# A fused Mamba-2 scan and gated feed-forward: three of Strassen's seven products placed between the first products of the next step

## The chip, the cores and the metric

The kernel runs on one core of a Trainium2 chip. The metric is the device time of one execution in microseconds (us); the median of three runs is used. A profile of one further execution shows each instruction on each engine: PE is TensorE's matmul, PEld its weight load, DVE VectorE, ACT ScalarE, POOL GpSimd, SP the queue that issues most transfers.

## The reference

Two blocks follow one another. The first is a chunked state-space scan (batch 4, 8 heads, 768 positions, head size 32, state size 16). Its output is laid out as 3072 tokens of 256 features and goes into a feed-forward block with a cosine gate:

```python
x = np.ascontiguousarray(attn_out.transpose(0, 2, 1, 3)).reshape(B * S, H * D)
h = x @ w_in             # (3072, 256) @ (256, 2048)
g = h * np.cos(h)
return (g @ w_out).astype(np.float32)   # (3072, 2048) @ (2048, 256)
```

All of it is fp32. The feed-forward block is nearly all of the matmul work, and the change lies in its second product.

## The kernel before

**Tiling.** The sequence is cut into 6 chunks of 128 positions (NC), so a chunk holds 4 x 128 = 512 tokens. The 2048 inner features are 16 blocks of 128 (NF). The main loop (L739) counts steps n, 16 a chunk and 96 in all, and two more to drain (LAG is 2). From chunk 1 on, a step takes half of the chunk's tokens (u = 0 or 1: 256 of them) and two of the inner blocks (a pair j of 8). So eight consecutive steps share one u, and build up one set of outputs.

**A step.** `first(n)` (L502) makes h for step n in one PSUM bank, `hp`: four products (L512), e for the two inner blocks and k for the two halves of the contraction, each a 128x128 stationary matrix against 256 moving columns. ScalarE then makes the whole turns `k` (L516) and VectorE the remainder `w` (L518), both issued in `first`; `gate(n)` lets ScalarE take the sine (L523), and `gated(n)` lets VectorE multiply (L528) into `gT`, which also frees `hp`. There are two `hp` banks. For the Strassen product GpSimd then makes four differences of gT's blocks in `differ` (L549): d0 and d1 by L553, d2 by L555, d3 by L556.

**The second product.** `second(n - LAG)` (L560) runs two steps later. In chunk 0 it is a plain product (L571). From chunk 1 on it calls `seven` (L581): gT is a 2x2 arrangement of 128x128 blocks (two token halves, two inner blocks), w_out's rows of the pair another (two inner blocks, two output halves), and Strassen's scheme in Winograd's form needs seven 128x128x128 products (L609) in place of eight. Products 1, 2 and 4 take gT's own blocks; product 3 takes d3, 5 takes d0, 6 takes d2, 7 takes d1. They come in the order 1, 2, 6, 7, 5, 4, 3, and each adds over the eight steps into a place of its own in two PSUM banks: 1, 6 and 2 in `lo`, 7, 5, 4 and 3 in `hi`. `start` is set for the first product in each bank, since it begins the bank anew.

**The accumulators.** Both banks are made anew at j = 0 from the tag "o", of which there are two. So the next set takes the banks of the one just finished, and each may be written only when its copy to SBUF is done: at j = 7 ScalarE copies `lo` (L618) and VectorE copies `hi` (L619), and GpSimd combines them in four additions (L624). The very last set lies in three banks (`mid`, `lo`, `hi`), and `shared` and `last_step` (L632, L644) finish it.

**What sets the order.** The program is scheduled by hand: each engine runs its instructions in the order in which the code issues them. In one turn of the loop that is `first(n)`, in some steps the scan's transposes (`turn2`), `gate`, `gated`, then `second(n - LAG)` with, at j = 7, the copies, and then the scan's work for the chunk to come (`intra2`, `finish2` on TensorE; `masked`, `decays`, `reaches` on VectorE). So TensorE runs four first products, then seven Strassen products; ScalarE runs k(n), the sine of n, and then the copy L618 where there is one; VectorE runs w(n), gT(n), the copy L619, then the scan.

Of the kernel before, what the change touches and what calls it, by code (L numbers as in the profile page):

```python
# [25 lines left out]
def kernel(  # L26
# [35 lines left out]
    NC = S // P  # L62
    DM, DF = moe_w_in.shape
    KT = DM // P
    NF = DF // P
# [4 lines left out]
    LAG = 2  # L70
# [15 lines left out]
    def bank(shape, name, tag):  # L86
        return psum.tile(shape, FP32, tag=tag, bufs=2, name=name)

    def pair(name):

        return psum.tile([P, 2, 4 * P], FP32, tag="scan", bufs=2, name=name)
# [405 lines left out]
    def turn_of(n):  # L497

        c, f = divmod(n, NF)
        return (f % 2, f // 2) if c == 0 else divmod(f, NJ)  # L500

    def first(n):  # L502
        c, f = divmod(n, NF)
        hp[n] = bank([P, TB], "hp", "h")

        u, j = turn_of(n)
        to_ = hp[n].rearrange("p (e t s i) -> p e t s i", e=2, t=2, s=2)
        y = yT[c].rearrange("p k (u s t i) -> p k u t s i", u=2, s=2, t=2)
        for e in range(2):
            fs = slice((2 * j + e) * P, (2 * j + e + 1) * P)  # L510
            for k in range(KT):
                PE.matmul(to_[:, e], lhsT=w_in[:, k, fs], rhs=y[:, k, u],  # L512
                          start=(k == 0), stop=(k == KT - 1), skip_group_check=True)

        k = ffn.tile([P, TB], I32, tag="k", name="k")
        ACT.activation(k, hp[n], AF.Copy, bias=0.25, scale=INV_2PI)  # L516
        turns[n] = w = ffn.tile([P, TB], FP32, tag="w", name="w")
        V.scalar_tensor_tensor(out=w, in0=hp[n], scalar=INV_2PI, in1=k,  # L518
                               op0=ALU.mult, op1=ALU.subtract)

    def gate(n):
        cos = turns[n]
        ACT.activation(cos, cos, AF.Sin, bias=quarter, scale=TWO_PI)  # L523
# [35 lines left out]

    def second(n):  # L560
        c, f = divmod(n, NF)
        if c > 0:
            seven(n)
            return
        u, j = turn_of(n)
        if j == 0:
            o[c, u] = bank([P, 2, DM], "o", "o")
        g = gT.pop(n)
        for e in range(2):
            for t in range(2):  # L570
                PE.matmul(o[c, u][:, t], lhsT=g[:, 2 * e + t], rhs=w_out[:, 2 * j + e],  # L571
                          start=(j == e == t == 0), stop=(j == NJ - 1 and e == 1),
                          skip_group_check=True)
        if j < NJ - 1:
            return
        ob = conv.tile([P, 2, DM], FP32, tag="last", bufs=3, name="ob")
        (ACT.copy if u else V.tensor_copy)(out=ob, in_=o[c, u])
        for s in range(2):
            nc.sync.dma_start(out=to_rows[2 * u + s, c], in_=ob[s * W:(s + 1) * W])

    def seven(n):  # L581

        c = n // NF
        u, j = turn_of(n)
        final = n >= NC * NF - NJ
        if j == 0:


            if final:
                lo, hi = (pair("o")[:, 0].rearrange("p (q m) -> p q m", m=P) for _ in range(2))  # L590
                mid = bank([P, 4, P], "o", "o")
                o[c, u] = (mid, lo, hi, {1: mid[:, 0], 6: mid[:, 1], 7: mid[:, 2], 5: mid[:, 3],
                                         2: lo[:, 0], 3: lo[:, 1], 4: hi[:, 0]})
            else:
                lo, hi = (bank([P, 4, P], "o", "o") for _ in range(2))
                o[c, u] = (lo, hi, {1: lo[:, 0], 6: lo[:, 1], 2: lo[:, 2], 7: hi[:, 0],
                                    5: hi[:, 1], 4: hi[:, 2], 3: hi[:, 3]})
        at = o[c, u][-1]
        g = gT.pop(n)
        if n == NC * NF - 1:  # L600
            last_step(g, *o[c, u][1:3])
            return
        d = gd.pop(n)
        w = {1: w4[:, j, 0, 0], 2: w4[:, j, 1, 0], 3: w4[:, j, 1, 1], 4: wd[3][:, j],
             5: wd[0][:, j], 6: wd[2][:, j], 7: wd[1][:, j]}
        a_ = {1: g[:, 0], 2: g[:, 2], 3: d[:, 3], 4: g[:, 3], 5: d[:, 0], 6: d[:, 2], 7: d[:, 1]}
        starts = (1, 2, 4) if final else (1, 7)
        for q in (1, 2, 6, 7, 5, 4, 3):
            PE.matmul(at[q], lhsT=a_[q], rhs=w[q], start=(j == 0 and q in starts),  # L609
                      stop=(j == NJ - 1), skip_group_check=True)  # L610
        if final and j == NJ - 2:
            shared(o[c, u][0])
        if j < NJ - 1:
            return

        sum_ = two.tile([P, 7, P], FP32, tag="sum", bufs=1, name="sum")
        ps = two.tile([P, 7, P], FP32, tag="ps", bufs=1, name="ps")
        ACT.copy(out=ps[:, 0:3], in_=o[c, u][0][:, 0:3])  # L618
        V.tensor_copy(out=ps[:, 3:7], in_=o[c, u][1])  # L619
        for dst, a_, b_ in ((sum_[:, 0:2], ps[:, 1:3], ps[:, 0:1]),  # L620
                            (sum_[:, 5:7], ps[:, 3:5], sum_[:, 0:1]),
                            (sum_[:, 3:5], ps[:, 5:3:-1], sum_[:, 5:6]),
                            (sum_[:, 2:3], ps[:, 6:7], sum_[:, 6:7])):
            G.tensor_tensor(out=dst, in0=a_, in1=b_.to_broadcast([P, dst.shape[1], P]), op=ALU.add)  # L624
        for s in range(2):
            nc.sync.dma_start(out=to_rows[2 * u + s, c],
                              in_=sum_[s * W:(s + 1) * W, 1:5].rearrange(
                                  "p (t h) m -> p t (h m)", t=2))
# [15 lines left out]
    def last_step(g, lo, hi):  # L644

        for t, acc in enumerate((lo, hi)):
            for e in range(2):
                PE.matmul(acc[:, 0:2], lhsT=g[:, 2 * e + t], rhs=w_out[:, NF - 2 + e],
                          start=False, stop=(e == 1), skip_group_check=True)
            ob = conv.tile([P, 2, P], FP32, tag="last", bufs=3, name="ob")  # L650
            V.tensor_tensor(out=ob, in0=acc[:, 0:2], in1=shares_[t], op=ALU.add)
            for s, eng in enumerate((nc.sync, nc.scalar)):
                eng.dma_start(out=to_rows[NB - 2 + s, NC - 1, :, t],
                              in_=ob[s * W:(s + 1) * W].rearrange("p h m -> p (h m)"))
# [54 lines left out]
    def first_scan():  # L709

        finish(3, "o")
        for u in range(2):
            sums[u] = pair("s_ps")[:, :, 0:2 * D]
            for t in range(2):
                sum_up(0, 2 * u + t, sums[u][:, t])
# [12 lines left out]
    def pairs(n):  # L728

        at = [(1 + (n - t) // NF, u) for u, t in enumerate(TURN) if (n - t) % NF == 0]  # L730
        return [(c, u) for c, u in at if 0 < c < NC]
# [7 lines left out]
    for n in range(NC * NF + LAG):  # L739
        c, f = divmod(n, NF)  # L740
        early = n < EARLY
        if n < NC * NF:
            if f == 0 and c > 0:
                load(c + 2)
            first(n)
            if n == 0:
                first_scan()
            for at in pairs(n):
                turn2(*at)
            rests = [grade(*piece[m], later=True)  # L750
                     for m in ((n,) if early else ()) + ((n + 1,) if n >= EARLY - 1 else ())
                     if m in piece]
            gate(n)
            for rest in rests:
                if rest:
                    rest()
            if not early and n in piece:
                join(*piece[n])
            gated(n)
            if early and n in piece:  # L760
                join(*piece[n])
            if n in (1, 2):
                carry(0, n - 1, sums[n - 1])
        for i, js in differ_at.get(n, ()):
            differ_w(i, js)
        if n >= LAG:
            second(n - LAG)
        for c, u in pairs(n - 1):
            intra2(c, u)
            masked(c, 2 * u)  # L770
        for c, u in pairs(n - 2):
            masked(c, 2 * u + 1)
        for c, u in pairs(n - 3):
            finish2(c, u)
            if u == 1:
                raw.pop(c)
        for c, b, t in halves_at(n):
            decays(c, b, t)
            if t == 1:
                load_a(c + 1, (b,))  # L780
        for c, u in pairs(n + 1):
            for b in (2 * u, 2 * u + 1):
                reaches(c, b)
                load_along(c + 1, (b,))
# [30 lines left out]
```

## Time and profile before

| | value |
|---|---|
| time, median of 3 runs | 387.14 us (386.27 to 387.29) |
| span of the profiled execution | 384.9 us |
| PE busy | 378.3 us, 2982 instructions |
| PEld busy | 331.2 us |
| DVE / ACT / POOL busy | 265.9 / 172.9 / 245.4 us |
| L512, first products | 768 instructions, 383 ns each |
| L609, Strassen products | 1106 instructions, 274 to 277 ns each |
| L553, L555, L556 GpSimd differences | 79 each; 911, 546, 455 ns |
| L516 k, L518 w, L523 sine, L528 gT | 96 each; 595, 681, 722, 691 ns |

An fp32 product is two matmul instructions and two weight loads, so four first products are eight instructions and seven Strassen products fourteen. The duration of a matmul instruction is longer than the distance to the next, since they are pipelined; distances are read from starts in the timeline or from the chain of waits, which counts each instruction up to the start of the next. In the chain each entry is what the one after it waited for or followed on its engine, traced back from the end.

### The profile page before, as it was taken

How to read it: one execution, taken by the hardware profiler on the slowest of the kernel's cores; microseconds unless marked ns; L12 is line 12 of the kernel's file. 1: busy time of each engine (PE TensorE's matmuls, PEld its weight loads, DVE VectorE, ACT ScalarE, POOL GpSimd, SP SyncE). 2: the span in 40 equal slices, each digit the busy share in tenths (PEclk: the TensorE clock that was granted, in tenths of full speed). 3: DMA queues.
4: the chain of work that ended last, by engine and by line, in shares of the span. 5: the costliest groups of instructions: out<-in, count | busy, mean ns of one | idle time of the engine just before them, and what ended most of it. 6: DMA issues, size and time to landing. Idle time of an engine off the chain costs nothing.

```text
span 384.9 us, 7726 instructions
## 1 busy us (share of the span) xinstructions
PE 378.3 (98%) x2982; PEld 331.2 (86%) x2982; DVE 265.9 (69%) x395; ACT 172.9 (45%) x303; POOL 245.4 (64%) x366
## 2 busy tenths in 40 slices
PE   8999999999999999999999999999999999999996
PEld 3578887888899899899899899899899989989995
DVE  7879999678667658657657757756765865863443
ACT  3878566534334334335334434434433433433441
POOL 5757665458859549648648837855955855853751
PEclk9999999999999999999999999999999999999999
DMA  7989899975002951301791301201210000010001
GB/s 83 270 235 266 249 230 137 181 96 151 2 0 63 148 52 57 96 2 54 127 81 55 97 2 56 81 17 43 68 43 1 21 10 0 2 27 3 7 22 27
DMA packets 106371, 30.42 MB, mean 79 GB/s; under 512 B 75520, under 2 KB 102240, under 8 KB 106336
## 3 DMA queue, kind: packets, MB, share of 16 engines
q1 hardware_dynamic: 106176, 29.81, 38.9%
q8 instruction: 23, 0.38, 0.5%
q10 hardware_dynamic: 160, 0.13, 0.1%
q14 instruction: 12, 0.10, 0.1%
HBM read 26.59 MB, written 3.34 MB: 78 GB/s over the span
## 4 chain that ended last, share of the span: by engine, by line
PE 82%; DVE 7%; POOL 3%; ACT 2%; issue 2%; DMA 2%; SPq 1%; ACTq 0%
PE hp L512 37%; PE o L609 32%; PE g L422 3%; PE y L454 3%; DVE mag L209 2%; DVE w L518 2%; DMA xr<-in_x_dram 2%; PE y L447 2%; DVE lam L344 2%; PE o L571 1%; DVE gT L528 1%; PE warm L101 1%; ACT w L523 1%; PE a_ps L298 1%; PE tp L405 1%
## 5 line engine op out<-in xcount | busy, mean ns | idle before, releaser
L512 PE MATMUL hp<-yT,w_in 128*128 128x256 f32 x768 | 184.4, 383 | 0.6 <-POOL w_in L217 0.3
L512 PEld LDWEIGHTS hp<-yT,w_in 128*128 128x128 f32 x768 | 139.2, 190 | 22.7 <-issue 4.5
L553 POOL TENSOR_TENSOR gd<-gT 128x256 f32<-128x256 f32 x79 | 71.9, 911 | 89.5 <-DVE gT L528 86.2
L528 DVE TENSOR_TENSOR gT<-hp,w 128x512 f32<-128x512 f32 x96 | 66.3, 691 | 69.9 <-ACT w L523 60.1
L523 ACT ACTIVATE w<-w,quarter 128x512 f32<-128x512 f32 x96 | 69.3, 722 | 97.2 <-DVE w L518 97.2
L516 ACT ACTIVATE k<-hp 128x512 int32<-128x512 f32 x96 | 57.1, 595 | 90.8 <-PE hp L512 90.7
L518 DVE SCALAR_TENSOR_TENSOR w<-hp,k 128x512 f32<-128x512 f32 x96 | 65.4, 681 | 36.7 <-ACT k L516 36.4
L609 PE MATMUL o<-words,gd 128*128 128x128 f32 x474 | 67.0, 277 | 0.6 <-POOL gd L555 0.6
L609 PEld LDWEIGHTS o<-words,gd 128*128 128x128 f32 x474 | 59.3, 192 | 2.4 <-POOL gd L555 2.2
L344 DVE TENSOR_TENSOR_SCAN lam<-arow,unit 128x512 f32<-128x512 f32 x40 | 55.7, 1394 | 0.0
L609 PEld LDWEIGHTS o<-w_out,gT 128*128 128x128 f32 x316 | 46.9, 191 | 3.6
L609 PE MATMUL o<-w_out,gT 128*128 128x128 f32 x316 | 48.0, 274 | 0.0
L555 POOL TENSOR_TENSOR gd<-gT,gd 128x128 f32<-128x128 f32 x79 | 43.1, 546 | 6.2
L556 POOL TENSOR_TENSOR gd<-gT,gd 128x128 f32<-128x128 f32 x79 | 35.9, 455 | 6.2
L571 PE MATMUL o<-w_out,gT 128*128 128x256 f32 x128 | 30.3, 380 | 0.4 <-POOL w_out L217 0.4
L609 PE MATMUL o<-w_out,gd 128*128 128x128 f32 x158 | 30.6, 275 | 0.0
L609 PE MATMUL o<-words,gT 128*128 128x128 f32 x158 | 30.5, 275 | 0.0
L571 PEld LDWEIGHTS o<-w_out,gT 128*128 128x128 f32 x128 | 24.2, 190 | 4.0 <-POOL w_out L217 0.8
L435 DVE TENSOR_TENSOR m<-g,lam 128x512 f32<-128x512 f32 x40 | 25.6, 681 | 0.0
L624 POOL TENSOR_TENSOR sum<-ps,sum 128x256 f32<-128x256 f32 (+1 forms) x27 | 24.2, 909 | 1.4
L609 PEld LDWEIGHTS o<-w_out,gd 128*128 128x128 f32 x158 | 24.0, 192 | 0.0
L609 PEld LDWEIGHTS o<-words,gT 128*128 128x128 f32 x158 | 24.0, 192 | 0.0
(91 smaller groups left out, 293.9 us busy)
## 6 DMA issues: line engine op xcount, KB each, us to landing
arow<-a_cut SPq DMA_DIRECT2D x20, 512.0 KB
words<-in_moe_w_in_dram SPq DMA_DIRECT2D x8, 512.0 KB
words<-in_moe_w_out_dram SPq DMA_DIRECT2D x8, 512.0 KB
out_dram<-sum SPq DMA_DIRECT2D x18, 128.0 KB
xr<-in_x_dram SPq DMA_DIRECT2D x4, 512.0 KB
along<-a_all SPq DMA_DIRECT2D x20, 64.0 KB
xr<-in_x_dram SPq DMA_DIRECT2D x8, 128.0 KB
bc<-in_B_dram SPq DMA_DIRECT2D x4, 256.0 KB
```

The lines of the kernel that those rows point to most:

```text
L344: V.tensor_tensor_scan(out=lam[c, b][:, hs].rearrange("p h i -> p (h i)"), data0=rows_.rearrange("p h i -> p (h i)"), data1=unit.rearrange ...
L435: V.tensor_tensor(out=of[0], in0=g[q][:, :, s * 2 * P:(s + 1) * 2 * P], in1=of[1], op=ALU.mult)
L512: PE.matmul(to_[:, e], lhsT=w_in[:, k, fs], rhs=y[:, k, u], start=(k == 0), stop=(k == KT - 1), skip_group_check=True)
L516: ACT.activation(k, hp[n], AF.Copy, bias=0.25, scale=INV_2PI)
L518: V.scalar_tensor_tensor(out=w, in0=hp[n], scalar=INV_2PI, in1=k, op0=ALU.mult, op1=ALU.subtract)
L523: ACT.activation(cos, cos, AF.Sin, bias=quarter, scale=TWO_PI)
L528: V.tensor_tensor(out=gT[n], in0=hp.pop(n), in1=cos, op=ALU.mult)
L553: G.tensor_tensor(out=d[:, 0:2], in0=g[:, 1:2].to_broadcast([P, 2, P]), in1=g[:, 3::-3], op=ALU.subtract)
L555: G.tensor_tensor(out=d[:, 2], in0=g[:, 0], in1=d[:, 0], op=ALU.subtract)
L556: G.tensor_tensor(out=d[:, 3], in0=g[:, 2], in1=d[:, 2], op=ALU.subtract)
L571: PE.matmul(o[c, u][:, t], lhsT=g[:, 2 * e + t], rhs=w_out[:, 2 * j + e], start=(j == e == t == 0), stop=(j == NJ - 1 and e == 1), skip_gr ...
L609: PE.matmul(at[q], lhsT=a_[q], rhs=w[q], start=(j == 0 and q in starts), stop=(j == NJ - 1), skip_group_check=True)
```

## The change

`seven` becomes a generator. It gives way after each of products 1, 2 and 4, which now come first; `first(n)` takes it as `between` and runs a part of it after its second, third and fourth product. So TensorE's order is: first products (e, k) = (0, 0), (0, 1), then product 1 of step n - 2, first product (1, 0), product 2, first product (1, 1), product 4. The parts left over (products 7, 5, 6, 3, and at j = 7 the copies and sums) run where `second` stood. The three products need only gT and weights, not GpSimd's differences of gT, and the order of the others changes too. Since product 4 is now the first in `hi`, `start` goes from 7 to 4. Making the new banks at j = 0 is in the generator's first part, so it comes between the first products as well. Steps of chunk 0 and the last two of the loop are not woven. The change is meant to keep TensorE in work with products that are ready early, and to ask later for those that wait for GpSimd.

```diff
-    def first(n):
+    def first(n, between=()):
+
+        between = iter(between)
...
                 PE.matmul(to_[:, e], lhsT=w_in[:, k, fs], rhs=y[:, k, u],
                           start=(k == 0), stop=(k == KT - 1), skip_group_check=True)
+                if e or k:
+                    next(between, None)
...
     def second(n):
         c, f = divmod(n, NF)
-        if c > 0:
-            seven(n)
-            return
...
-        starts = (1, 2, 4) if final else (1, 7)
-        for q in (1, 2, 6, 7, 5, 4, 3):
+        starts = (1, 2, 4) if final else (1, 4)
+        for q in (1, 2, 4, 7, 5, 6, 3):
             PE.matmul(at[q], lhsT=a_[q], rhs=w[q], start=(j == 0 and q in starts),
                       stop=(j == NJ - 1), skip_group_check=True)
+            if q in (1, 2, 4):
+                yield
...
-            first(n)
+            weave = seven(n - LAG) if n - LAG >= NF else iter(())
+            first(n, weave)
...
-        if n >= LAG:
+        if LAG <= n < NF + LAG:
             second(n - LAG)
+        else:
+            for _ in weave if n < NC * NF else seven(n - LAG):
+                pass
```

## The prediction

> **What bounds the kernel now.** I read the page's shares first, then the chain of waits in the Strassen stretch, the list of waits, and the timeline of one place where the accumulators change hands. From the page:
>
> ```profile
> PE 378.3 (98%) x2982; PEld 331.2 (86%) x2982; DVE 265.9 (69%) x395; ACT 172.9 (45%) x303; POOL 245.4 (64%) x366
> ...
> PE 82%; DVE 7%; POOL 3%; ACT 2%; issue 2%; DMA 2%; SPq 1%; ACTq 0%
> ```
>
> TensorE is busy for 98% and is 82% of the chain. From the chain of waits between 200 and 260 us (start, us, what):
>
> ```profile
> 237.22 1.73 PE hp L512 x8
> 238.95 1.56 PE o L609 x14
> ...
> 244.24 1.73 PE hp L512 x8
> 245.97 1.81 PE o L609 x14
> ```
>
> One step is 8 first-product instructions in 1.73 us (216 ns each) and 14 Strassen instructions in 1.56 us (111 ns each; the fp32 product is two instructions), 3.29 us together with no hole. The second pair holds the only kind of hole: 1.81 for 14 instructions, 0.25 too many. The list of waits names it (us in total, times, longest):
>
> ```profile
> PEld o L609 <- POOL gd L555: 2.2, 9, 0.8
> PE o L609 <- POOL gd L555: 0.6, 1, 0.6
> ```
>
> These are waits of product 6, third of the seven, for GpSimd's second difference. Every wait also costs the pipelining of the next pair: six instructions of L609 take 0.94 us after one, 0.83 without, so 0.1 us is added. By the timeline the holes are 0.83 us at 94.5, 0.25 at seven later places (125, 155, 185, 246, 277, 307, 337), 0.28 at 209 (this one is for VectorE's copy L619) and 0.31 at 216: 0.83 + 1.75 + 0.59 = 3.17 us. That is all that there is to win.
>
> Now the place where one set of accumulators is emptied and the next is begun (timeline, start us, us, engine):
>
> ```profile
> 235.76 0.60 ACT L516 ACTIVATE k<-hp 128x512 int32<-128x512 f32 x1 [1.21 <-PE hp L512]
> ...
> 236.39 0.69 DVE L518 SCALAR_TENSOR_TENSOR w<-hp,k 128x512 f32<-128x512 f32 x1
> ...
> 237.06 1.89 PE L512 MATMUL hp<-yT,w_in 128*128 128x256 f32 x8
> ...
> 237.12 0.72 ACT L523 ACTIVATE w<-w,quarter 128x512 f32<-128x512 f32 x1 [0.76 <-DVE w L518]
> ...
> 237.74 0.46 ACT L618 COPY ps<-o 128x384 f32<-128x384 f32 x1
> ...
> 238.55 0.68 DVE L619 COPY ps<-o 128x512 f32<-128x512 f32 x1
> ...
> 238.79 0.61 PE L609 MATMUL o<-w_out,gT 128*128 128x128 f32 x4
> ```
>
> ScalarE's copy L618 empties the first bank at 238.20, and the next product 1 needs that bank at 238.79. So the wait is hidden today, with 0.59 us to spare, only because the whole of `first` stands ahead of product 1. The second bank is free at 239.23, after product 1 has begun: each bank is waited for by itself. There are nine such places:
>
> ```profile
> L618 ACT COPY ps<-o x9: 457/460/461, 116.2 to 358.5; 128x384 f32<-128x384 f32 x9
> ```
>
> **What the skill says.** "TensorE: Matmul & The Clock Gate", section "Step-by-step: what each phase is for": matmuls keep program order and only weight loads are pulled ahead; so first products behind a waiting product wait too. The trace agrees: behind the late product 6 everything slips. The same page, "LDWEIGHTS (loading the stationary operand)", gives columns/1.2 ns, an estimate of 107 ns for 128 columns; the trace has 111 ns per small instruction, so these are already at the pace of the loads. "Perfetto Trace Analysis", "Tensor Engine Instruction (MATMUL, LD_WEIGHTS)", calls ScalarE and VectorE strict FIFO: the copy L618 can't pass the sine L523 ahead of it, and the trace shows it 0.62 us after that sine's start at every place.
>
> **The change part by part.**
>
> *Weaving by itself.* The same 22 instructions per step, the same loads. A small one costs 111 ns beside small ones, a large one 216. In the timeline of single starts the first small one after a large one is 109 after it began, the first large one after small ones 218: two more changes of size a step are -3 + 2 ns each, under 0.2 us over 78 steps. I take zero.
>
> *Products 1 and 2 inside `first`.* They put 2 x 2 x 111 = 0.446 us ahead of the last first product, so hp ends 0.446 us later in its step, and so do k, w, sine, gT and GpSimd's differences of that step. These have slack in the steady state: gT frees hp at 237.94 + 0.69 = 238.63 by the same timeline, and the bank is written again two steps after 233.77, at 240.35: 1.7 us to spare.
>
> *The accumulators' handover.* Before, product 1 came after 8 large instructions; now after 4, at 237.06 + 0.86 = 237.92. The copy L618 comes 0.446 later, since k, w and the sine ahead of it in ScalarE's and VectorE's queues do: it ends at 238.20 + 0.45 = 238.65. A product starts some 0.05 us after its releaser ended (GpSimd 215.59 + 0.46 = 216.05, product at 216.10). So product 1 starts at 238.70: a hole of 0.78 us, and 0.1 for the lost pipelining, 0.88. Behind it in TensorE's queue stand the other half of `first` and all that follows, and nothing takes up the hole. Nine times: 7.9 us. Product 4, first into the second bank, comes some 1.4 us after product 1, at 240.1; copy L619 ends at 239.23 + 0.45 = 239.68, so no second hole. With no latency the hole is 0.73, with 0.2 us of latency and pipelining apart 1.03: 6.6 to 9.3 us.
>
> *The first woven step* has its first bank free, but product 4 needs the bank of L577 (ScalarE, 86.23 + 0.57 = 86.79) at 84.61 + 1.73 + 0.45 = 86.79: about 0.15 us lost.
>
> *The new order 1, 2, 4, 7, 5, 6, 3.* Product 6 moves from 1.73 + 0.45 = 2.17 us into the step to 2.17 + 3 x 0.22 = 2.84, 0.67 later, while the differences are 0.45 later: 0.22 us more slack, against waits of 0.15 to 0.21. Product 7 comes 0.22 later than product 6 did, and needs the difference of L553, which is ready 0.53 (0.45 of L555 and a gap) before that of L555: 0.3 more. At the wait of 94.5 GpSimd is held by L547, not by the shifted chain; there the move is worth 0.67 to product 6 and more to 7. So I take all 3.17 us as won.
>
> *The end.* `last_step` waits for gT(95), whose chain starts at the last first product's end: 0.446 later, and all behind it: 0.45 us lost. Product 6's later place delays the shared sums by 0.22 us, beside `last_step`'s 1.9 us of products: nothing.
>
> Sum: 7.9 + 0.15 + 0.45 - 3.17 = +5.3 us; 387.14 + 5.3 = 392.5 us.
>
> **The rivals.**
>
> 1. *No new hole* (the bank is free early enough after all, if ScalarE's copy moved ahead or the wait were taken elsewhere): only the gain, 387.14 - 3.17 + 0.6 = 384.6, or 384.0 if the end is hidden too. For it: 0.59 us of slack today. Against it: the product moves up by 0.86 us and the copy down by 0.45. Chance 0.14; this is the side of faster.
> 2. *A half hole*: the chain's shift is taken up somewhere (k, w and sine of that step not later). Hole 0.78 - 0.45 + 0.1 = 0.43, nine times 3.9: 387.14 + 3.9 + 0.6 - 3.17 = 388.5. Against it: k starts 0.1 us after the last first product, w and sine 0.03 us after their inputs, so there is no slack to take it up. Chance 0.08.
> 3. *The old waits stay* (VectorE and GpSimd slow each other: L553 is 0.72 to 1.58 us): the holes cost 8.5 and nothing is won, 395.7. Chance 0.08.
> 4. *Product 1 waits for both banks*: until L619 at 239.68 + 0.05, a hole of 1.8 + 0.1, nine times 17: about 401.8. Against it: product 1 at 238.79 did not wait for L619's end at 239.23. Chance 0.05.
>
> **How the numbers follow.** My forecast has 0.65, its bounds (6.6 to 9.3 us, gains half lost) 390.5 to 395.5. The range 388.3 to 396.0 takes in rivals 2 and 3 and leaves out 1 and 4. Faster 0.14, from rival 1; same 0.04, from between rivals 1 and 2; slower 0.82.
>
> **What would show it.** In the trace of after: the list of waits should name TensorE's L609 waiting for ACT ps L618 nine times, about 0.8 us each, and the chain should run through L523 and L618 there; the waits for L555 should be gone; a woven step without a handover should take 3.29 us as before; `last_step` should wait some 0.45 us. I am wrong if the handover shows no hole, or if steps between handovers are no longer 3.29 us, as they would be if alternating sizes changed the pace of the loads.

## The result, and the profile after

The changed kernel takes 391.68 us (median of 4 runs, 391.33 to 392.77) against 387.07 us for the kernel before on the same occasion: 1.0127 times as long, with a 95% interval of 1.0102 to 1.0153, which is 3.9 to 5.9 us. The forecast was 392.5.

From the page of the changed kernel, its shares of the span and the chain by engine:

```profile
PE 377.9 (97%) x2982; PEld 329.9 (85%) x2982; DVE 266.6 (68%) x395; ACT 174.9 (45%) x303; POOL 245.3 (63%) x366
...
PE 67%; DVE 14%; ACT 9%; issue 4%; DMA 3%; SPq 2%; POOL 0%; DVEq 0%; ACTq 0%
```

The instructions and TensorE's busy time are those of before, but TensorE is now 67% of the chain and not 82%; ScalarE has gone from 2% to 9% and VectorE from 7% to 14%. GpSimd, 3% before, is out of it. The list of waits of the changed kernel (total, times, longest) says which wait came in:

```profile
PEld o L611 <- ACT ps L622: 9.1, 9, 1.0
...
PE o L611 <- ACT ps L622: 5.5, 9, 0.6
```

L611 is what was L609, L622 what was L618. Nine waits, one for each set of accumulators that is emptied; the waits for GpSimd's L555 (now L559) are gone from the list; one of 0.2 us for L560, the difference of product 3, is new. One of the nine in the timeline of the changed kernel (start us, us, engine), at the same step as the place shown of before:

```profile
237.13 0.60 ACT L520 ACTIVATE k<-hp 128x512 int32<-128x512 f32 x1 [1.21 <-PE hp L514]
...
237.76 0.69 DVE L522 SCALAR_TENSOR_TENSOR w<-hp,k 128x512 f32<-128x512 f32 x1
...
237.99 1.03 PE L514 MATMUL hp<-yT,w_in 128*128 128x256 f32 x4
...
238.49 0.72 ACT L527 ACTIVATE w<-w,quarter 128x512 f32<-128x512 f32 x1 [0.76 <-DVE w L522]
...
239.11 0.46 ACT L622 COPY ps<-o 128x384 f32<-128x384 f32 x1
...
239.63 0.49 PE L611 MATMUL o<-w_out,gT 128*128 128x128 f32 x2 [0.61 <-ACT ps L622]
...
239.92 0.68 DVE L623 COPY ps<-o 128x512 f32<-128x512 f32 x1
...
240.38 0.38 PE L611 MATMUL o<-w_out,gT 128*128 128x128 f32 x2
```

Two first products (four instructions) end their turn at 237.99 + 4 x 0.216 = 238.86; product 1 starts at 239.63, since the copy ends at 239.57. VectorE's copy L623 ends only at 240.60, so it is not the one that product 1 waited for. The hole is 0.77 us, and the pair takes 0.49 and not 0.38: 0.88 in all.

Where the time went can be read from starts in the timeline, step by step (a step reaches from one first product's start to the next one's). I take it from step 18, the first that is woven, to TensorE's end:

| part | before to after, us |
|---|---|
| eight handovers, 3.29 to 4.17 each | +7.04 |
| the ninth (step 50), 3.57 to 4.24, of which 0.28 was there before | +0.67 |
| step 18 | +0.21 |
| from the start of step 95 to TensorE's end, 6.91 to 7.36 | +0.45 |
| step 20, 5.28 to 4.71 | -0.57 |
| eight steps two after a handover (28, 36, ... 84): seven of -0.24 to -0.26, one of -0.31 | -2.06 |
| sum; measured 296.58 to 302.27 | +5.74; +5.69 |

All other steps have their old length. The 5.7 us stand beside 4.6 in the medians and 4.7 in the two profiled spans, because step 18 began at 83.67 us in the profile of after and at 84.62 in that of before. The code up to there is the same, and in the profiles of all kernels below that start lies between 83.67 and 85.18. The scatter comes from the very beginning: from step 0 to step 18 each of these nine profiles takes 65.82 to 65.86 us, while step 0 begins between 17.85 and 19.32. The first matmuls of the program (L101, six that multiply ones) show it, before and then after:

```profile
1.06 4.63 PE L101 MATMUL warm<-ones 128*128 128x512 f32 x6 [1.06 <-DVE ones L96]
...
1.06 3.89 PE L101 MATMUL warm<-ones 128*128 128x512 f32 x6 [1.06 <-DVE ones L96]
```

In both, the second and third start 853 or 854 ns before the next; the fifth starts 426 ns before the sixth in the first profile and 217 in the second, so there TensorE had come to twice the pace sooner. I therefore compare the kernels from step 18 on where the difference is small.

### The profile page after: what moved, and what is told of

Same layout as the page of the kernel before. It is cut to its first block, busy times and chain, and to the rows that moved or that the text cites. A ratio compares the mean times of both kernels' runs of the same rounds, so it can differ in the third digit from the quotient of the medians.

```text
span 389.6 us, 7726 instructions
## 1 busy us (share of the span) xinstructions
PE 377.9 (97%) x2982; PEld 329.9 (85%) x2982; DVE 266.6 (68%) x395; ACT 174.9 (45%) x303; POOL 245.3 (63%) x366
## 4 chain that ended last, share of the span: by engine, by line
PE 67%; DVE 14%; ACT 9%; issue 4%; DMA 3%; SPq 2%; POOL 0%; DVEq 0%; ACTq 0%
PE hp L514 29%; PE o L611 23%; DVE lam L344 6%; DVE w L522 5%; ACT w L527 5%; PE g L422 3%; PE o L572 3%; PE y L454 3%; SPq L119 2%; ACT k L520 2%; PE y L447 2%; DMA words<-in_moe_w_out_dram 1%; DVE gT L532 1%; DMA arow<-a_cut 1%; PE tp L405 1%
## 5 line engine op out<-in xcount | busy, mean ns | idle before, releaser
L514 PE MATMUL hp<-yT,w_in 128*128 128x256 f32 x768 | 210.3, 383 | 0.6 <-POOL w_in L217 0.3
L514 PEld LDWEIGHTS hp<-yT,w_in 128*128 128x128 f32 x768 | 127.3, 191 | 14.6 <-issue 4.2
L611 PEld LDWEIGHTS o<-w_out,gT 128*128 128x128 f32 x316 | 59.1, 190 | 16.7 <-ACT ps L622 9.1
L611 PE MATMUL o<-w_out,gT 128*128 128x128 f32 x316 | 61.5, 277 | 5.5 <-ACT ps L622 5.5
L611 PE MATMUL o<-words,gd 128*128 128x128 f32 x474 | 65.8, 275 | 0.0
L611 PEld LDWEIGHTS o<-words,gd 128*128 128x128 f32 x474 | 59.3, 192 | 0.0
L559 POOL TENSOR_TENSOR gd<-gT,gd 128x128 f32<-128x128 f32 x79 | 43.1, 546 | 6.2
L560 POOL TENSOR_TENSOR gd<-gT,gd 128x128 f32<-128x128 f32 x79 | 35.9, 455 | 6.2
L611 PEld LDWEIGHTS o<-words,gT 128*128 128x128 f32 x158 | 29.8, 190 | 4.5 <-issue 0.4
L611 PE MATMUL o<-w_out,gd 128*128 128x128 f32 x158 | 30.6, 276 | 0.0
L611 PE MATMUL o<-words,gT 128*128 128x128 f32 x158 | 30.5, 275 | 0.0
L572 PEld LDWEIGHTS o<-w_out,gT 128*128 128x128 f32 x128 | 24.2, 190 | 4.0 <-POOL w_out L217 0.8
L611 PEld LDWEIGHTS o<-w_out,gd 128*128 128x128 f32 x158 | 24.0, 192 | 0.2 <-POOL gd L560 0.2
```

The source lines that it names most:

```text
L514: PE.matmul(to_[:, e], lhsT=w_in[:, k, fs], rhs=y[:, k, u], start=(k == 0), stop=(k == KT - 1), skip_group_check=True)
L559: G.tensor_tensor(out=d[:, 2], in0=g[:, 0], in1=d[:, 0], op=ALU.subtract)
L560: G.tensor_tensor(out=d[:, 3], in0=g[:, 2], in1=d[:, 2], op=ALU.subtract)
```

## The experiments

The theory: the order of ScalarE's queue (the copy stands behind the sine) makes the nine holes; weaving as such costs nothing; the new order of the products brings the gain. The rivals: weaving small products between large ones costs by itself; another wait takes the hole's place; the gain comes from the weaving.

**The copies ahead of the sine.** In the changed kernel, at j = 7, the rest of the products and the two copies are issued before `gate(n)`, the sums where they were:

```diff
         V.tensor_copy(out=ps[:, 3:7], in_=o[c, u][1])
+        yield
...
                 turn2(*at)
+            if n - LAG >= NF and turn_of(n - LAG)[1] == NJ - 1:
+                next(weave)
```

> The woven kernel, with the two copies that empty a finished set of accumulators issued ahead of that step's sine, not behind it; weaving and order of products as in the changed kernel. If ScalarE's order is the cause (the copy stands behind the sine), all nine holes of 0.88 us go: 391.7 - 8.0 = 383.7 us, and TensorE's L609/L611 waits for ps vanish from the list of waits. If alternating product sizes cost something by themselves, or another wait (the second bank) takes the hole's place, it stays above 387.

Measured: 385.89 us, ratio to before 0.9981 (0.9971 to 0.9990), where before took 386.53. The timeline of this kernel at the same handover, ScalarE, then TensorE:

```profile
236.10 0.48 ACT L622 COPY ps<-o 128x384 f32<-128x384 f32 x1 [0.23 <-PE o L611]
236.63 0.72 ACT L527 ACTIVATE w<-w,quarter 128x512 f32<-128x512 f32 x1
...
236.13 1.03 PE L514 MATMUL hp<-yT,w_in 128*128 128x256 f32 x4
236.99 0.38 PE L611 MATMUL o<-w_out,gT 128*128 128x128 f32 x2
```

The copy ends at 236.58, product 1 starts at 236.99, straight after two first products (four instructions). All nine holes are gone: step 26 takes 3.29 us, and with it every handover. So the first half of the theory holds: taking the copies from behind the sine removes the holes, and woven steps without a hole are as long as unwoven ones. The edit moves both copies; that ScalarE's is the one that counts follows from the list of waits and the timeline of the changed kernel above.

But I expected 383.7, and the second half has failed: of the 2.06 us won at the steps two after a handover, only 0.40 is left (0.03 to 0.06 each, once 0.12). GpSimd's timeline of this kernel around such a step, then TensorE's:

```profile
240.83 0.73 POOL L629 TENSOR_TENSOR sum<-ps 128x256 f32<-128x256 f32 x1
241.64 2.87 POOL L629 TENSOR_TENSOR sum<-ps,sum 128x256 f32<-128x256 f32 x3
244.47 0.72 POOL L557 TENSOR_TENSOR gd<-gT 128x256 f32<-128x256 f32 x1
245.28 0.46 POOL L559 TENSOR_TENSOR gd<-gT,gd 128x128 f32<-128x128 f32 x1
245.81 0.46 POOL L560 TENSOR_TENSOR gd<-gT,gd 128x128 f32<-128x128 f32 x1
...
245.54 0.83 PE L611 MATMUL o<-words,gd 128*128 128x128 f32 x6
246.32 0.49 PE L611 MATMUL o<-w_out,gd 128*128 128x128 f32 x2
```

Product 3, the last of the seven, starts at 246.32, when L560 has made its difference at 246.27; six instructions of 0.11 from 245.54 would have let it start at 246.21. The four sums (3.6 us) stand ahead of the differences in GpSimd's queue, without a pause from 240.83 on. In the changed kernel the hole of 0.88 gave GpSimd that time. The same step there, GpSimd and then TensorE:

```profile
247.79 0.46 POOL L560 TENSOR_TENSOR gd<-gT,gd 128x128 f32<-128x128 f32 x1
...
248.95 0.39 PE L611 MATMUL o<-w_out,gd 128*128 128x128 f32 x2
```

L560 is done at 248.25, 0.70 us ahead of product 3. Two steps earlier TensorE had lost 0.88; without that, by this estimate, the difference would have come 0.18 after the product's turn.

**The order alone.** The kernel before, with nothing woven:

```diff
-        starts = (1, 2, 4) if final else (1, 7)
-        for q in (1, 2, 6, 7, 5, 4, 3):
+        starts = (1, 2, 4) if final else (1, 4)
+        for q in (1, 2, 4, 7, 5, 6, 3):
```

> The kernel before with the new order 1, 2, 4, 7, 5, 6, 3 alone, nothing woven. If the gain comes from the order: of the 2.9 us of waits for GpSimd some 2.5 go (one of 0.35 stays in the first Strassen steps), but product 4, now third, meets the copy of the second bank: 0.15 at seven handovers, 0.2 more at one and 0.15 at the first step, 1.4 us back: 387.1 - 2.5 + 1.4 = 386.0 us. If the gain came from the weaving, about 387.1 or 388.5.

Measured: 385.64 us, ratio 0.9977 (0.9969 to 0.9985). By steps: the whole gain of after is there, 0.57 at step 20 and 2.06 at the eight others, and seven handovers have 0.15 each (0.22 at step 50, 0.23 at step 18, none at step 90, where the very last set begins) for product 4, which now comes third and meets the copy of the second bank. TensorE's timeline of this kernel at one handover, then VectorE's copy:

```profile
238.14 0.61 PE L609 MATMUL o<-w_out,gT 128*128 128x128 f32 x4
238.63 0.49 PE L609 MATMUL o<-words,gT 128*128 128x128 f32 x2
...
237.90 0.68 DVE L619 COPY ps<-o 128x512 f32<-128x512 f32 x1
```

The copy ends at 238.58; product 4 would have started at 238.14 + 4 x 0.11 = 238.58 and starts at 238.63. From step 18 to the end this kernel has 295.44 us, 1.14 less than before. With nothing woven all of the gain is there, so it belongs to the order, not to the weaving.

**Nothing woven where a set begins.** The changed kernel with

```diff
-            first(n, weave)
+            first(n, weave if turn_of(n - LAG)[1] else ())
```

> The changed kernel, with nothing woven in the steps that begin a set of accumulators (j = 0). Product 1 then comes after all of first and finds its bank free (some 0.1 us to spare), but product 4 comes third and meets VectorE's copy of the second bank, which the woven step before has delayed by 0.45: seven holes of 0.58 and one of 0.95 in place of nine of 0.88, 5.0 for 8.0: 391.7 - 3.0 = 388.7 us. If only ScalarE's copy mattered: 383.7.

Measured: 389.46 us, ratio 1.0075 (1.0057 to 1.0094). From the list of waits of this kernel:

```profile
PE o L611 <- DVE ps L623: 2.9, 8, 0.7
```

TensorE's matmuls no longer wait for ScalarE's copy, and eight waits for VectorE's have come instead: step 26 takes 3.89 us, seven handovers have 0.60 and step 50 has 0.95. I had expected 0.58 and 0.95. The weights of product 1 still wait a little for ScalarE's copy (0.2 us at most), and its second instruction comes 0.014 late. So it isn't enough to take product 1 out of `first`: since the step before is woven, both copies come 0.45 us late (at one handover VectorE's starts 1.93 us into the step, and 1.49 in the kernel before), and the next product that needs a bank runs into the second.

**One first product sooner.** The changed kernel with its three products after the first, second and third of `first`:

```diff
-                if e or k:
+                if not (e and k):
```

> The changed kernel with each woven product one first product sooner (after the first, second and third, so that all three lie ahead of hp's end). Product 1 is due 0.43 us sooner and the copy that it waits for comes 0.22 later: each of nine holes grows by 0.65 to 1.54, 5.9 us more, the end 0.2 more and the first woven step 0.4: 391.7 + 6.5 = 398.2 us. If weaving itself cost time, and not the handover, no change: 391.7.

Measured: 398.06 us, ratio 1.0297 (1.0277 to 1.0317). From its list of waits:

```profile
PE o L611 <- ACT ps L622: 11.4, 9, 1.3
...
PE o L652 <- DVE gT L532: 0.6, 1, 0.6
```

Each handover grows from 0.88 to 1.54 (step 26: 4.83 us), as worked out: 0.43 because product 1 is due sooner and 0.22 because the third product stands ahead of hp's end too. The end grows in the same way: from step 95 to TensorE's end 6.91 us with nothing woven, 7.36 with two products ahead of hp's end, 7.58 with three, 0.22 for each. Step 20, where the changed kernel kept a wait of 0.25, has none here (4.46 us): the hole two steps earlier, at step 18, is larger (0.64 and not 0.21) and gave GpSimd the time.

**The new order except where a set begins.** The kernel before, with

```diff
-        for q in (1, 2, 6, 7, 5, 4, 3):
+        for q in (1, 2, 4, 7, 5, 6, 3) if j else (1, 2, 6, 7, 5, 4, 3):
```

> The kernel before, nothing woven, with the new order of the seven products in all steps but those that begin a set of accumulators (j = 0), which keep the old one. If the order alone buys the gain, it keeps what the order-only kernel won at GpSimd's waits (0.57 at step 20, 0.25 to 0.31 at eight more, 2.6 us) and loses the waits for the banks that it had got in exchange (0.15 at seven handovers, 0.22 and 0.23 at two): 386.5 - 2.6 = 383.9 us. If weaving were needed for the gain: 385.6 or more.

Measured: 384.57 us, ratio 0.9956 (0.9943 to 0.9969), where before took 386.14. The handovers are as before, the eight steps keep their 2.06, step 20 keeps 0.36 (with 0.23 lost at step 18 it won 0.57, so it also lived on a hole). From step 18 on: 294.16, 2.42 less than before. The medians show only 1.57 of this, and the median is 0.7 above the 383.9 that I expected; the start of the program scatters by more than that.

**The same with the copies ahead of the sine.**

```diff
         V.tensor_copy(out=ps[:, 3:7], in_=o[c, u][1])
+        yield
...
+            if n - LAG >= NF and turn_of(n - LAG)[1] == NJ - 1:
+                next(weave)
```

(here `seven` has no other `yield`, and `first` gets nothing to weave)

> As the order-by-step kernel, and with the two copies ahead of the sine as well. Only the hole of 0.28 at step 50, where product 7 met the copy of the second bank, is left to win: 386.5 - 2.9 = 383.6 us, the same within the measurement as order-by-step. If the copies ahead of the sine harm the gate's chain: above 384.5.

Measured: 384.57 us, ratio 0.9958 (0.9943 to 0.9973). The 0.28 at step 50 are won, and 0.04 at each of the eight steps lost, where the difference for product 3 comes just in time for its first instruction and its second slips by that much. From step 18 on 294.23, so gain and loss cancel. The copies ahead of the sine are not free here: where a set is finished the sine starts 0.29 us later than in order-by-step, and with it gT and GpSimd's sums, which is where the eight losses come from. My bound of 384.5 doesn't decide, since order-by-step has the same median.

**The sums one step later.** The woven kernel with the copies ahead of the sine, and at j = 7 the rest of the generator (the sums and their transfers) kept for the next turn of the loop (`late` starts out empty):

```diff
         else:
-            for _ in weave if n < NC * NF else seven(n - LAG):
+            for _ in late:
+                pass
+            rest = weave if n < NC * NF else seven(n - LAG)
+            late = rest if turn_of(n - LAG)[1] == NJ - 1 and n < NC * NF else iter(())
+            for _ in () if turn_of(n - LAG)[1] == NJ - 1 and n < NC * NF else rest:
                 pass
```

> The woven kernel with the copies ahead of the sine, and GpSimd's four sums of a finished set issued one step later, behind the differences of that step. The copies-first kernel kept waits of 0.2 at eight steps two after a handover, for the third difference, which GpSimd made late because the woven step hands it gT 0.45 later and the sums (3.6 us) stand ahead. If so they go: 385.9 - 1.7 = 384.2 us, with the end's 0.45 the only price of the weave left. If the wait comes from the scan on VectorE or from GpSimd's pace with it, it stays near 385.9.

Measured: 383.78 us, ratio 0.9940 (0.9927 to 0.9952). GpSimd's timeline of this kernel, then TensorE's, around the same step:

```profile
240.04 1.51 POOL L557 TENSOR_TENSOR gd<-gT 128x256 f32<-128x256 f32 x1 [0.71 <-DVE gT L532]
241.62 0.45 POOL L559 TENSOR_TENSOR gd<-gT,gd 128x128 f32<-128x128 f32 x1
242.16 0.46 POOL L560 TENSOR_TENSOR gd<-gT,gd 128x128 f32<-128x128 f32 x1
242.57 0.72 POOL L629 TENSOR_TENSOR sum<-ps 128x256 f32<-128x256 f32 x1
...
244.00 0.83 PE L611 MATMUL o<-words,gd 128*128 128x128 f32 x6
244.67 0.39 PE L611 MATMUL o<-w_out,gd 128*128 128x128 f32 x2
```

The difference for product 3 is ready at 242.62, two microseconds before its use, and product 3 follows without a wait. All 2.06 us are back. From step 18 on the kernel has 294.30 us, 2.28 less than before: what it still pays for the weave is 0.21 at step 18 and 0.45 at the end. It beats the kernel before and the changed kernel. Against order-by-step (294.16) it is the same from step 18 on; its lower median goes with a start that was 0.75 us shorter in its profile.

## Why the prediction was right, point by point

**The handover** was right in mechanism and size: nine holes, 0.78 + 0.1 forecast, 0.77 + 0.11 measured, through the copy behind the sine. The copies-first kernel takes them to nothing, the one-sooner kernel to 1.54. Product 4 had no second hole; only at step 50, where gT and with it VectorE's copy are later than elsewhere, did its second instruction slip by 0.07. I had taken all nine for alike.

**Weaving by itself** was put at zero. A woven step with no handover has 3.29 us, as before.

**The first woven step**: 0.15 forecast, 0.21 measured, of the kind described: product 4 was 0.14 late and its second instruction 0.07 more.

**The end**: 0.45 forecast, 0.45 measured, and in proportion to the products ahead of hp's end.

**The new order** is where a step failed, although its sum came out near (3.17 forecast, 0.57 + 2.06 + 0.28 = 2.91 measured, of which the 0.28 at step 50 is counted within its handover in the table). The step was "0.22 us more slack, against waits of 0.15 to 0.21. [...] So I take all 3.17 us as won". I had looked at products 6 and 7 and not at product 3, which stays last: the new order gives it nothing, and the chain that is 0.45 later takes from it. At step 20 it kept a wait of 0.25. At the eight steps after handovers it would have waited too, as the copies-first kernel shows (0.4 us won instead of 2.06); in the changed kernel the hole of 0.88, two steps earlier, gave GpSimd the time to be ready. The terms of my sum were not independent: part of the gain was paid for by the loss. That this term came near was luck: 1.66 of the 2.91 us were there only because of the holes.

**The rivals.** No hole, half a hole and a wait for both banks are out: the hole had its full size and ended 0.05 us after ScalarE's copy, well before VectorE's. "The old waits stay" was wrong for the changed kernel. Without the holes most of the gain at the eight steps is indeed lost, but to other waits and for another reason than that rival gave: product 3 waits, not product 6, and GpSimd's differences took no longer than before there (0.72, 0.46 and 0.46 us) but stood behind the sums.

One slip of arithmetic in the forecast's bounds: with holes of 6.6 us the sum gives 391.2, not the 390.5 named as the lower bound.

What stays open: why TensorE's first matmuls come to their full pace at a different time in each execution, which moves the whole program by up to 1.5 us.

## What to carry to other kernels

Moving work forward on a full engine gains nothing unless it fills a hole, and it moves every buffer's deadline forward too: look for the step in which the buffer changes hands, not at the steady step, and follow the release through the queue of the engine that makes it. Work put ahead of a producer also delays all that hangs on that producer by the same amount, here the copy, the differences and the end of the kernel. When a loss and a gain lie two steps apart in one pipeline, don't add them as if each stood alone: a hole on one engine is slack for the others, and closing it can bring a wait back.

## What the runs showed of the hardware that was not expected

A wait of an fp32 product costs more than its length: after nearly every one, whoever released it, the second instruction of the pair came 213 to 214 ns after the first and not 111 or 112, some 0.1 us on top. So a wait of 0.05 us costs 0.15, as the seven short handovers of the order-only kernel did. It was seen with ScalarE, VectorE and GpSimd as releaser. The exception is product 4 at step 18: in the six kernels in which it waited, the second instruction came 184 or 185 ns after the first.

The starts of the weight loads (PEld) show which distance stays the same. A product that waited did not have its weights loaded ahead, even where it waited only for its bank: at the handover shown of the changed kernel, L622's copy ends at 239.57 and both the load and the first instruction start at 239.62 to 239.63. At all waits with a full 213 or 214 ns the load started 51 to 53 ns after its releaser had ended. In the nine profiles 89 pairs of the seven products have a second instruction that came late (more than 114 ns after the first), and at each of them it came 215 or 216 ns after the start of the first load, whether the first instruction was late or not. So it can slip alone: at eight steps of the order-and-copies kernel the difference for product 3 was ready at 244.69, its load started at 244.74, the first instruction was on time at 244.80, and only the second was late, by 0.045 us.
